# Bucketed attention and a wide feed-forward block on one core: the keyless share in the values' bank, a sum kept in PSUM, first products ahead of block transposes, and a hand-ordered last part

## The chip, the core and the metric

One core of one Trainium2 chip runs the whole program. The metric is device microseconds of one execution. TensorE (PE) multiplies, VectorE (DVE) and ScalarE (ACT) do elementwise work and read PSUM, GpSimd (POOL) works on SBUF alone, SyncE (SP) issues most DMAs. Each engine works through its own queue in order; waits between engines are semaphores.

## What is computed

Attention over 4 batches, 8 heads, 768 positions, head size 64, in which a query sees only the keys of its own hash bucket (six sign bits of a projection); then, with the heads joined to rows of 512, a normalised feed-forward block with 2048 hidden units and a residual.

```python
q_bits = (np.einsum('bhsd,dk->bhsk', q, proj) > 0)
k_bits = (np.einsum('bhsd,dk->bhsk', k, proj) > 0)
mask = q_bucket[:, :, :, None] == k_bucket[:, :, None, :]
scores = np.where(mask, scale * (q @ k.T), -1e9)
attn = np.exp(scores - max); attn = attn / (attn.sum(-1) + 1e-09)
x = heads_joined(attn @ v)
xn = (x - mu) / np.sqrt(var + 1e-06) * g_ln
out = x + np.maximum(xn @ w_ch1, 0.0) @ w_ch2
```

A query whose bucket holds no key sees all keys with equal weight (every score is -1e9). That is the share of keyless queries: the kernel gives every key a weight of 2^-100 beside the masked exponentials, which counts only where nothing else does.

## The kernel before

The work is cut into 12 chunks of 256 query rows (4 batches by 3). A chunk has two stages.

**Attention.** `att_units` (line 417) makes 12 units for a chunk: four pairs of heads, three units each. A unit is `scores` (S: 4 matmuls, line 446, into a two-bank tile of `ps_sc`, two of them), `exps` (one ACT instruction, line 456), `values` (A: 8 matmuls with the values and a column of ones, line 480, into the pair's tile `av`) and, after a pair's third unit, `divide` (lines 489 to 510) on DVE. The tile `av` is one bank of `ps_av`, and pairs take its two tags `av0` and `av1` in turn. For batch 0 the keyless share enters by a matmul (line 469). For batches 1 to 3 it is a tile `vsum` that `divide` adds: line 500 reads the sums of weights, line 501 adds `vsum` to the bank's numerators and writes the result to the SBUF tile `x`, line 506 takes the reciprocal, line 508 multiplies `x` by it in place.

**Feed-forward.** `mlp_steps` (line 516): `norm` (statistics with lines 527 and 528, centring with line 529, for the two row blocks in turn; then one DMA transpose on SP's queue, line 549, makes `xnT`), eight `up` steps (U: 8 matmuls, line 577, into a tile `hp`, then a rectification that goes to DVE, line 587, and ACT, line 589, by turns) and eight `down` steps (D: 4 matmuls, line 618; every fourth is followed by the residual on DVE, line 623, and the write of 128 rows). The tiles `hp`, `o2`, `hash` and `share` all take turns in the two banks of `ps_mm`: a new one waits until the reader of the one before last is done.

**Preparing the later batches**, by halves of four heads, on letters of a plan: L and W load, N casts to bfloat16 on POOL, B is four block transposes on DVE (line 287), T a DMA transpose, H the hash products (line 321), J spreads the bits by DMA, P shifts rows by DMA, V casts the values and sums them on POOL (lines 351 to 360), E is `share` (line 362): one matmul of the sums `vs16` into a bank of `ps_mm`, and a DVE copy into `vsum`.

**The order.** Chunks 0 and 1 are in a long list written out by hand. For chunks 2 to 11 the words of `steps[n]` (or `plain`) order the norm (`n`), the D steps (`d`), the U steps (`u`) and the preparation around the 12 units: chunk n's units run beside the norm and the U steps of chunk n-1 and the D steps of chunk n-2. `interleave` (line 692) places S of the next unit, then filler steps, then A, then fillers; a step's cost (U 900, D 870, H 1300, E 110, most others 0) decides where it lands. What costs 0 moves nothing on PE.

After chunk 11's units there remain the norm of chunk 11, eight D steps of chunk 10, eight U and eight D steps of chunk 11, the last four D steps split in two halves of columns (`down_columns`, line 596). That part is outside `manual_schedule`, so a scheduler orders each engine's queue. At the end each engine loads a flag (line 902) and branches (line 903) over a general path that these inputs do not need.

Of the kernel before, what the change touches and what calls it, by code (L numbers as in the profile page):

```python
# [9 lines left out]
F32 = mybir.dt.float32  # L10
# [20 lines left out]
def kernel(  # L31
# [11 lines left out]
    nc = tc.nc  # L43
    P = 128
# [102 lines left out]
    def load_values(b, half):  # L147
        h0 = half * H // 2
        eng = nc.gpsimd if (b, half) == (1, 0) else nc.sync
        if (b, half) == (0, 1):  # L150

            t = work.tile([P, NH * CT // 2], F32, tag="h", bufs=1, name="vnat1")[
                :, 0 : H // 2 * NC * D
            ].rearrange("p (h c d) -> p h c d", h=H // 2, c=NC)
        else:
            t = nat.tile([P, H // 2, NC, D], F32, tag="vnat", bufs=1, name="vnat")
        eng.dma_start(
            out=t, in_=v[b, h0 : h0 + H // 2].rearrange("h (p c) d -> p h c d", p=P)
        )
        return t  # L160

    class Prep:

# [197 lines left out]

        def share(self, half):

            ps = ps_mm.tile([P, H // 2 * D], F32, tag="mm", name="share")
            nc.tensor.matmul(ps, epsk, self.vs16.rearrange("p h d -> p (h d)"))
            nc.vector.tensor_copy(
                self.vs[:, half * H // 2 : (half + 1) * H // 2].rearrange("p h d -> p (h d)"), ps
            )
# [48 lines left out]
    def att_units(b, t, x):  # L417
# [15 lines left out]
        for j in range(NP):  # L433
            ha, hb = 2 * j, 2 * j + 1
            groups = [
                [(ha, 0), (ha, 1), (ha, 2), (ha, 3)],
                [(ha, 4), (ha, 5), (hb, 4), (hb, 5)],
                [(hb, 0), (hb, 1), (hb, 2), (hb, 3)],
            ]
            state = {}  # L440
            for g, grp in enumerate(groups):

                def scores(grp=grp, g=g, state=state):
                    sc = ps_sc.tile([P, 4, CT], F32, tag="sc", name="sc")
                    for i, (h, kj) in enumerate(grp):
                        nc.tensor.matmul(  # L446
                            sc[:, i, :],
                            key_block(h, kj),
                            query_blocks(h),
                        )  # L450
                    state["sc", g] = sc

                def exps(g=g, state=state):
                    sc = state["sc", g]
                    ex = work.tile([P, 4, CT], BF16, tag="ex", bufs=3, name="ex")
                    nc.scalar.activation(  # L456
                        ex, sc, AF.Exp,
                        bias=expb[:, 1:2] if b else expb[:, 0:1],
                        scale=scale if b else scale / Q_SCALE,
                    )  # L460
                    state[g] = ex

                def values(grp=grp, g=g, state=state, j=j, ha=ha):
                    if g == 0:
                        slot = 0 if (b, t) == (0, 0) else j % 2
                        av = ps_av.tile([P, 2, TT, D1], F32, tag=f"av{slot}", name="av")
                        state["av"] = av
                        if b == 0:
                            nc.tensor.matmul(
                                av,  # L470
                                epsk,
                                vsplit[:, ha : ha + 2, :].unsqueeze(2).to_broadcast(
                                    [P, 2, TT, D1]
                                ),
                                start=True, stop=False, skip_group_check=True,
                            )
                    av = state["av"]
                    for i, (h, kj) in enumerate(grp):
                        for qi in range(TT):
                            nc.tensor.matmul(  # L480
                                av[:, h - ha, qi, :],
                                state[g][:, i, qi * P : (qi + 1) * P],
                                va[:, h, kj, :],
                                start=(b > 0 and (g, i, qi) == (0, 0, 0)),
                                stop=(g == 2 and i == 3),
                                skip_group_check=True,
                            )

                def divide(g=g, state=state, ha=ha):
                    if g == 2:  # L490
                        av = state["av"]
                        rc = work.tile([P, 2, TT], F32, tag="rc", name="rc")
                        xv = x[:, :, ha * D : (ha + 2) * D].rearrange(
                            "p t (h d) -> p h t d", h=2
                        )
                        num = av[:, :, :, 0:D]
                        if b == 0:
                            nc.vector.reciprocal(rc, av[:, :, :, D])
                        else:
                            nc.vector.tensor_scalar_add(rc, av[:, :, :, D], S * EPS_KEY)  # L500
                            nc.vector.tensor_tensor(  # L501
                                xv, num,
                                vs[:, ha : ha + 2, :].unsqueeze(2).to_broadcast([P, 2, TT, D]),
                                op=AOP.add,
                            )
                            nc.vector.reciprocal(rc, rc)
                            num = xv
                        nc.vector.tensor_tensor(  # L508
                            xv, num, rc.unsqueeze(3).to_broadcast([P, 2, TT, D]), op=AOP.mult
                        )  # L510

                units.append((scores, exps, values, divide))
# [3 lines left out]
    def mlp_steps(b, t, x):  # L516
        st = {}
        steps = []

        def norm_rows(i):  # L520

            if i == 0:
                st["xn"] = work.tile([P, ND, TT, P], BF16, tag="xn", bufs=1, name="xn")
                st["mv"] = work.tile([P, TT, 2], F32, tag="mv", name="mv")
            xn, mv = st["xn"], st["mv"]
            stats = work.tile([P, 6], F32, tag="stats", bufs=4, name="stats")
            nc.vector.bn_stats(stats, x[:, i, :])  # L527
            nc.vector.bn_aggr(mv[:, i, :], stats)  # L528
            nc.vector.scalar_tensor_tensor(  # L529
                xn[:, :, i, :],  # L530
                x[:, i, :].rearrange("p (o d) -> p o d", d=P),
# [10 lines left out]

        def norm():

            for i in range(TT):
                norm_rows(i)
            if b or t > 1:
                xnT = work.tile([P, ND, CT], BF16, tag="xnT", bufs=1, name="xnT")
                nc.sync.dma_start_transpose(
# [17 lines left out]
            st["xnT"] = work.tile([P, ND, CT], BF16, tag="xnT", bufs=1, name="xnT")  # L567
            nc.vector.tensor_copy(st["xnT"], st["tp"])

        def up_products(n2):  # L570
            if n2 == 0:
                st["h"] = work.tile([P, NH, CT], BF16, tag="h", bufs=1, name="hbuf")
            hp = st["hp", n2] = ps_mm.tile([P, 2, CT], F32, tag="mm", name="hp")
            for i in range(2):
                nt = 2 * n2 + i
                for dt in range(ND):
# [36 lines left out]
        def down(i, part):  # L613
# [20 lines left out]
            (870, lambda i=i, part=part: down(i, part)) for i in range(TT) for part in range(4)  # L634
        ]
        parts = {
            "rows": norm_rows, "scale": norm_scale, "xt": xtrans, "xe": xcopy,
            "up": up_products, "relu": rectify, "columns": down_columns,
        }

# [106 lines left out]
    def first_two():  # L747
# [32 lines left out]
        def both(i):  # L780
# [22 lines left out]
            "su": lambda half: prep.sum_products(half),  # L803
            "sd": lambda half: prep.split_sums(half),
            "w": loads,
            "n": lambda i: parts["rows"](i),
            "nr": lambda _: parts["scale"](),
            "xt": lambda _: parts["xt"](),
            "xe": lambda _: parts["xe"](),
# [15 lines left out]

    steps = {
# [8 lines left out]
    }  # L835
    plain = "n d d d d d d d d u u u u u u u u"
    singly = {
# [9 lines left out]
    def sequence(text, norm, downs, ups, xtrans):  # L847

        downs, ups, out = list(downs), list(ups), []
        for word in text.split():  # L850
# [15 lines left out]
                out.append(parts_left[word].pop(0))  # L866
            else:
                out += prepare(word)
        assert not downs and not ups
        return out  # L870

    with tc.manual_schedule():
# [19 lines left out]
            interleave(units[n], fillers, after, single)  # L892
    tc.no_sync_barrier()
    norm, ups, downs, _, parts = mlp_steps(*chunks[-1], xs[len(chunks) - 1])
    for _, f in [norm] + tail + ups + downs[: 4 * (TT - 1)]:
        f()
    for lo in range(0, d_model, d_model // 2):
        parts["columns"](TT - 1, lo, lo + d_model // 2)
    main.close()


    ok = nc.values_load(flag[0:1, 0:1], min_val=0, max_val=1)
    with tc.If(ok < 1):
        general_path(
            tc, q, k, v, proj1, gbc, n_bits, w1_sb, w2_sb, identf, ident, out,
        )
# [192 lines left out]
```

## Time and profile before

| | us |
|---|---|
| median of 3 runs | 314.43 (313.21 to 315.44) |
| the profiled execution | 312.45 |
| its span, first to last instruction | 310.6 |

| engine | busy us | share of the span |
|---|---|---|
| PE | 299.4 | 96% |
| ACT | 217.2 | 70% |
| DVE | 184.6 | 59% |
| POOL | 84.7 | 27% |

Chunk 2's units begin at about 50 us, chunk 11's end at 285.7. The granted clock of PE is 1.0 throughout. The view of stages shows how full each engine is where the change acts (columns: us, then busy time of PE, its weight loads, DVE, ACT, POOL; granted clock; DMA share; GB/s):

```profile
core 0: us, PE busy (x) PEld busy (x) DVE busy (x) ACT busy (x) POOL busy (x), PEclk, DMA share, GB/s
75.00:98.00 23.00, 22.56 (x244) 17.32 (x244) 14.77 (x32) 18.13 (x24) 8.10 (x10) 1.00 0.62 168
98.00:123.00 25.00, 24.72 (x287) 18.86 (x288) 15.52 (x34) 19.45 (x27) 8.84 (x10) 1.00 0.55 139
171.00:195.00 24.00, 23.67 (x271) 17.89 (x273) 16.47 (x35) 18.30 (x25) 9.28 (x10) 1.00 0.57 133
285.70:310.60 24.90, 21.24 (x142) 13.80 (x142) 9.72 (x19) 2.76 (x5) 1.71 (x2) 1.00 0.19 57
```

### The profile page before, as it was taken

Reading aid. Unit: us, or ns where it says so; the run is one execution under the profiler, and the core shown is the slowest. Engines: PE = TensorE matmul, PEld = TensorE weight load, DVE = VectorE, ACT = ScalarE, POOL = GpSimd, SP = SyncE. Lnnn points to the kernel's source line nnn. Section 1 sums busy time; section 2 is a strip of 40 time slices with the busy share of each in tenths; the row PEclk is TensorE's granted clock in tenths of the full one; section 3 lists DMA queues with packets and bytes.
Section 4 is the critical chain, followed back from the end, with each engine's and each line's share of the span. In section 5 each row is a group of like instructions: output and inputs, shape, how many; then the busy total and the mean of one; then the engine's idle time right before and its main releaser. Section 6 shows DMA issues by size and latency. Waiting matters only on the chain.

```text
span 310.6 us, 7810 instructions
## 1 busy us (share of the span) xinstructions
PE 299.4 (96%) x3241; PEld 226.0 (73%) x3268; DVE 184.6 (59%) x404; ACT 217.2 (70%) x272; POOL 84.7 (27%) x110
## 2 busy tenths in 40 slices
PE   7979999999999999999999999999999999999995
PEld 6656787678669678678679668669679678688574
DVE  1799996654665756743793694653643734734522
ACT  5677977775798777688788778778778677666020
POOL 3467530914321118151290470100100100100200
PEclk9999999999999999999999999999999999999999
DMA  7999998487396476695199637030030110200302
GB/s 237 374 208 304 211 339 129 103 124 185 52 313 156 93 245 119 130 273 154 64 262 154 171 76 168 19 76 37 1 102 0 35 71 0 69 36 0 104 0 77
DMA packets 64970, 40.93 MB, mean 132 GB/s; under 512 B 47153, under 2 KB 59953, under 8 KB 64929
## 3 DMA queue, kind: packets, MB, share of 16 engines
q1 hardware_dynamic: 60224, 31.59, 41.1%
q0 software_dynamic: 4128, 8.13, 11.1%
q10 hardware_dynamic: 576, 0.66, 0.6%
q8 instruction: 27, 0.44, 0.6%
q14 instruction: 15, 0.11, 0.1%
HBM read 27.98 MB, written 6.88 MB: 112 GB/s over the span
## 4 chain that ended last, share of the span: by engine, by line
PE 84%; DVE 9%; ACT 3%; issue 2%; DMA 1%; POOL 0%; SPq 0%; ACTq 0%; POOLq 0%
PE hp L577 26%; PE o L618 22%; PE sc L446 18%; PE av L480 10%; PE hash L321 3%; DVE slots L262 2%; PE tpose L200 1%; DVE slots L238 1%; DVE bt L287 1%; PE wakep L762 1%; PE o L600 1%; PE hash L252 1%; DMA xnT<-xn 1%; DVE xn L529 1%; DVE x L508 1%
## 5 line engine op out<-in xcount | busy, mean ns | idle before, releaser
L456 ACT ACTIVATE ex<-sc,expb 128x1024 bf16<-128x1024 f32 x144 | 159.5, 1113 | 56.5 <-PE sc L446 54.0
L577 PE MATMUL hp<-xnT,w_sb 128*128 128x256 bf16 x768 | 98.7, 272 | 1.6 <-DVE hbuf L587 0.9
L618 PE MATMUL o<-w_sb,hbuf 128*128 128x512 bf16 x341 | 89.6, 379 | 1.2
L446 PE MATMUL sc<-slots 70*128 70x256 bf16 x576 | 86.5, 272 | 2.2 <-POOL slots L238 1.5
L577 PEld LDWEIGHTS <-w_sb 128*128 128x128 bf16 x768 | 72.0, 97 | 11.2 <-issue 2.4
L480 PEld LDWEIGHTS <-ex 128*128 128x128 bf16 x1152 | 54.0, 98 | 15.7 <-ACT ex L456 1.6
L446 PEld LDWEIGHTS <-slots 70*128 70x128 bf16 x576 | 51.8, 97 | 17.2 <-issue 3.7
L480 PE MATMUL av<-vaug,ex 128*128 128x65 bf16 x1152 | 58.8, 194 | 0.3 <-ACT ex L456 0.2
L587 DVE TENSOR_SCALAR hbuf<-hp 128x512 bf16<-128x512 f32 x48 | 32.8, 684 | 43.6 <-PE hp L577 42.5
L618 PEld LDWEIGHTS <-hbuf 128*128 128x128 bf16 x368 | 33.6, 97 | 25.5
L540 POOL TENSOR_SCALAR rs<-mv 128x2 f32<-128x2 f32 x12 | 9.1, 759 | 155.2 <-DVE mv L528 155.2
L589 ACT ACTIVATE hbuf<-hp 128x512 bf16<-128x512 f32 x48 | 28.5, 594 | 20.2 <-PE hp L577 20.2
L623 DVE SCALAR_TENSOR_TENSOR x<-o,rs,x 128x512 f32<-128x512 f32 x23 | 17.1, 744 | 26.4 <-PE o L618 23.5
L529 DVE SCALAR_TENSOR_TENSOR xn<-x,mv,gbc 128x512 bf16<-128x512 f32 x24 | 17.9, 751 | 0.8
L508 DVE TENSOR_TENSOR x<-x,rc 128x256 f32<-128x256 f32 x36 | 16.8, 466 | 1.2
L500 DVE TENSOR_SCALAR rc<-av 128x4 f32<-128x4 f32 x36 | 5.7, 158 | 19.8 <-PE av L480 19.8
L527 DVE BATCH_NORM_STATS2 stats<-x 128x6 f32<-128x512 f32 x24 | 16.5, 690 | 0.4
L351 POOL CAST vaug<-vnat 128x1536 bf16<-128x1536 f32 x8 | 12.0, 1494 | 15.6 <-DMA vnat<-in_v_dram 15.6
L501 DVE TENSOR_TENSOR x<-av,vsum 128x256 f32<-128x256 f32 x36 | 14.9, 414 | 0.0
L282 POOL CAST nat<-qnat 128x1536 bf16<-128x1536 f32 x6 | 8.8, 1470 | 16.8 <-issue 8.8
L180 ACT ACTIVATE knat<-knat 128x768 f32<-128x768 f32 x16 | 13.4, 836 | 0.0
L180 ACT ACTIVATE qnat<-qnat 128x768 f32<-128x768 f32 x16 | 13.3, 833 | 0.0
(86 smaller groups left out, 215.9 us busy)
## 6 DMA issues: line engine op xcount, KB each, us to landing
out_dram<-x SPq DMA_DIRECT2D x23, 256.0 KB
vnat<-in_v_dram SPq DMA_DIRECT2D x7, 768.0 KB
qnat<-in_q_dram SPq DMA_DIRECT2D x11, 384.0 KB
knat<-in_k_dram SPq DMA_DIRECT2D x11, 384.0 KB
w_sb<-in_moe_w_ch_dram POOLq DMA_DIRECT2D x4, 1024.0 KB, 14.4
slots<-slots SPq DMA_DIRECT2D x6, 384.0 KB
qnat<-in_q_dram POOLq DMA_DIRECT2D x2, 768.0 KB, 14.8
knat<-in_k_dram POOLq DMA_DIRECT2D x2, 768.0 KB, 16.0
```

Of the source, the lines that this page charges most:

```text
L180: nc.scalar.activation(src, src, AF.Square, accum_out=sq[:, a, col : col + 1],)
L446: nc.tensor.matmul(sc[:, i, :], key_block(h, kj), query_blocks(h),)
L456: nc.scalar.activation(ex, sc, AF.Exp, bias=expb[:, 1:2] if b else expb[:, 0:1], scale=scale if b else scale / Q_SCALE,)
L480: nc.tensor.matmul(av[:, h - ha, qi, :], state[g][:, i, qi * P : (qi + 1) * P], va[:, h, kj, :], start=(b > 0 and (g, i, qi) == (0, 0, 0)) ...
L508: nc.vector.tensor_tensor(xv, num, rc.unsqueeze(3).to_broadcast([P, 2, TT, D]), op=AOP.mult)
L527: nc.vector.bn_stats(stats, x[:, i, :])
L529: nc.vector.scalar_tensor_tensor(xn[:, :, i, :], x[:, i, :].rearrange("p (o d) -> p o d", d=P), mv[:, i, 0:1], gbc.rearrange("p (o d) -> p ...
L577: nc.tensor.matmul(hp[:, i, :], w1_sb[:, dt, nt * P : (nt + 1) * P], st["xnT"][:, dt, :], start=(dt == 0), stop=(dt == ND - 1),)
L587: nc.vector.tensor_scalar_max(dst, src, 0.0)
L589: nc.scalar.activation(dst, src, AF.Relu)
L618: nc.tensor.matmul(o2, st["h"][:, nt, i * P : (i + 1) * P], w2_sb[:, nt, :], start=(nt == 0), stop=(nt == NH - 1),)
L623: nc.vector.scalar_tensor_tensor(x[:, i, :], o2, st["rs"][:, i : i + 1], x[:, i, :], op0=AOP.mult, op1=AOP.add,)
```

## The change

Six edits:

1. `share` writes its product into the `av` tag that the latest pair does not hold, not into `ps_mm`.
2. For batches 1 to 3 the sum of numerators and `vsum` is written back to the PSUM bank and multiplied from there; `x` is written once.
3. In the plans of chunks 3, 4 and 7 some U steps stand ahead of the block transposes B; chunk 11 leaves its eighth U step out of the interleaving.
4. The norm is split into `row_stats` and `row_centred`, and for the last chunk both statistics come before both centrings.
5. The last part is ordered by hand: first the products of chunk 10's eighth U step, then the last norm, then the D steps of chunk 10, then the eight U steps, of which every second takes its tile from `ps_sc`, so that four are there.
6. A branch hint (LikelyTaken) is put on DVE and ACT for the branch over the general path. In the queues it stands behind chunk 11's last division on DVE and ahead of the last five rectifications on ACT.

PE's queue has the same instructions; up to chunk 10 they stand in the same order. On DVE, line 501's successor now waits for line 500's successor (both use the bank), the reciprocal no longer waits, and in the last norm the order is statistics, aggregate, statistics, aggregate, centring, centring, where the scheduler had put both statistics ahead of both aggregates. The queues of POOL and SP are unchanged.

```diff
         def share(self, half):
-            ps = ps_mm.tile([P, H // 2 * D], F32, tag="mm", name="share")
+            ps = ps_av.tile([P, H // 2 * D], F32, tag=f"av{1 - pair_bank[-1]}", name="share")
...
                         av = ps_av.tile([P, 2, TT, D1], F32, tag=f"av{slot}", name="av")
+                        pair_bank.append(slot)
...
                             nc.vector.tensor_tensor(
-                                xv, num,
+                                num, num,
                                 vs[:, ha : ha + 2, :].unsqueeze(2).to_broadcast([P, 2, TT, D]),
                                 op=AOP.add,
                             )
                             nc.vector.reciprocal(rc, rc)
-                            num = xv
...
-            for i in range(TT):
-                norm_rows(i)
+            if (b, t) == (B - 1, NT - 1):
+                order = [(row_stats, 0), (row_stats, 1), (row_centred, 0), (row_centred, 1)]
+            else:
+                order = [(row_stats, 0), (row_centred, 0), (row_stats, 1), (row_centred, 1)]
+            for step, i in order:
+                step(i)
...
-        def up_products(n2):
+        def up_products(n2, wide=False):
...
-            hp = st["hp", n2] = ps_mm.tile([P, 2, CT], F32, tag="mm", name="hp")
+            pool, tag = (ps_sc, "sc") if wide and n2 % 2 else (ps_mm, "mm")
+            hp = pool.tile([P, 2, CT], F32, tag=tag, name="hp")
+            st["hp", n2] = hp
...
-        3: "n L20 d d d d W20 d E11 d N20 d N20 B20 d T20 B20 u B20 u B20 u P20 u u u u u",
-        4: "n L21 d d d H20 d J20 d d N21 d N21 B21 d T21 B21 V20 u B21 u B21 u P21 W21 u u u u u",
+        3: "n L20 d d d d W20 d E11 d N20 d N20 B20 d T20 u B20 u u B20 u u B20 P20 u u u",
+        4: "n L21 d d d H20 d J20 d d N21 d N21 B21 d T21 V20 u B21 u u B21 u u B21 P21 W21 u u u",
...
-        7: "n d d d H30 d J30 N31 d N31 B31 d T31 B31 E30 d B31 V31 d B31 u P31 u u u u u u u",
+        7: "n d d d H30 d J30 N31 d N31 B31 d T31 B31 E30 d B31 V31 d u B31 u P31 u u u u u u",
...
+        11: "n d d d d d d d d u u u u u u u",
...
-    for _, f in [norm] + tail + ups + downs[: 4 * (TT - 1)]:
-        f()
-    for lo in range(0, d_model, d_model // 2):
-        parts["columns"](TT - 1, lo, lo + d_model // 2)
+    held = mlp[len(chunks) - 2][4]
+    with tc.manual_schedule():
+        held["up"](NH // 2 - 1)
+        norm[1]()
+        held["relu"](NH // 2 - 1, nc.scalar)
+        for _, f in tail:
+            f()
+        for n2 in range(NH // 2):
+            parts["up"](n2, True)
+            parts["relu"](n2, nc.scalar if n2 % 2 else nc.vector)
+        for _, f in downs[: 4 * (TT - 1)]:
+            f()
+        tc.mark_branch_hint_location(
+            "general", "LikelyTaken", [nc.vector.engine, nc.scalar.engine]
+        )
+        for lo in range(0, d_model, d_model // 2):
+            parts["columns"](TT - 1, lo, lo + d_model // 2)
...
-    with tc.If(ok < 1):
+    with tc.If(ok < 1, label="general"):
```

More of the change, by code (lines that the diff above doesn't have):

```diff
@@ L160, in load_values @@
         return t
+    pair_bank = []
     class Prep:
@@ L518, in mlp_steps, with row_stats @@
         steps = []
-        def norm_rows(i):
+        def row_stats(i):
             if i == 0:
@@ L524, in norm_rows @@
                 st["mv"] = work.tile([P, TT, 2], F32, tag="mv", name="mv")
-            xn, mv = st["xn"], st["mv"]
+            mv = st["mv"]
             stats = work.tile([P, 6], F32, tag="stats", bufs=4, name="stats")
@@ L528, in norm_rows, with row_centred @@
             nc.vector.bn_aggr(mv[:, i, :], stats)
+        def row_centred(i):
+            xn, mv = st["xn"], st["mv"]
             nc.vector.scalar_tensor_tensor(
@@ L636, in mlp_steps @@
         parts = {
-            "rows": norm_rows, "scale": norm_scale, "xt": xtrans, "xe": xcopy,
+            "stats": row_stats, "centred": row_centred, "scale": norm_scale, "xt": xtrans, "xe": xcopy,
             "up": up_products, "relu": rectify, "columns": down_columns,
@@ L805, in first_two @@
             "w": loads,
-            "n": lambda i: parts["rows"](i),
+            "n": lambda i: (parts["stats"](i), parts["centred"](i)),
             "nr": lambda _: parts["scale"](),
@@ L868, in sequence @@
                 out += prepare(word)
-        assert not downs and not ups
+        assert not downs
         return out
```

## The prediction

> **What bounds the kernel now.** I read the page's busy times first, then the chain of waits over the whole span, then the places where the chain leaves PE. PE is busy 96% of the span at a granted clock of 1.0. The chain gives prices for work that doesn't wait: a U step (8 products) 0.87 us, a D step (4) 0.86, S (4) 0.43, A (8) 0.26. A U step that starts later than its predecessors' prices allow is a stall. Five places before the last part show one (columns: start, us, what):
>
> ```profile
> 70.93 0.70 DVE hbuf L587
> 71.67 1.03 PE hp L577 x8
> ...
> 92.03 0.66 DVE hbuf L587
> 92.74 1.03 PE hp L577 x8
> ...
> 113.94 0.89 DVE bt L287
> 115.38 0.96 DVE bt L287
> 116.97 1.03 PE hp L577 x8
> ...
> 142.35 1.11 ACT ex L456
> 144.00 1.03 PE hp L577 x8
> ...
> 184.39 0.89 DVE bt L287
> 185.84 0.96 DVE bt L287
> 187.42 1.03 PE hp L577 x8
> ```
>
> Each time a U step waits for a rectification that frees its bank, and at 116.97 and 187.42 that rectification stood behind block transposes (92.74 likewise: the timeline has a transpose at 91.13 for 0.98 ahead of the rectification at 92.03). The sixth stall is in the last part, where the norm of chunk 11 outlasts the D steps that cover it:
>
> ```profile
> 286.80 1.29 DVE stats L527 x2
> 288.22 1.41 DVE xn L529 x2
> 289.69 3.07 DMA xnT<-xn
> 292.81 7.44 PE hp L577 x64
> ```
>
> Summing over starts of consecutive matmuls from 45 us on, what exceeds these prices and isn't a missing record comes to some 2.5 us. That is about all that PE can win there.
>
> **The share in the values' bank.** Before, the share's bank comes between two U tiles, so the next U waits for the last one's rectification. Six shares are made; the timeline shows two that cost time, at 70.98 and 143.66, both right after a pair's last A.
> - 70.98: the share takes 0.11 (the pace of 0.87/8), so U could start at 71.09, not 71.67: 0.58 won. But the bank that the share now takes is the next pair's. That pair's first matmul (line 469) would come at 71.09+0.87+0.43 = 72.39; the copy to vsum ends at 72.09+0.41 = 72.50, and PE starts 0.05 after a DVE release (71.62 to 71.67). So 0.16 goes back: net -0.42.
> - 143.66: U could start at 143.77, not 144.00: 0.23 won. The next pair's A would then come at 144.64; the copy ends at 144.79, 0.115 later by the slower division below, so A starts at 144.95: 0.31 lost. Net +0.08. Behind that A in PE's queue wait a U and the next S, so all of PE waits, ACT with its unit of slack does not.
> - The other four lie inside a pair, with at least one A step and 1.5 us ahead of the next pair: 0.
>
> **The sum in PSUM.** 36 divisions change. The add must now wait for line 500, which reads the same bank. Before, the two overlap (285.72 for 0.16, then 285.80); a waiting instruction starts 0.035 after its predecessor's end (line 506 ends at 286.30, line 508 starts at 286.34). So 0.16+0.035-0.08 = 0.115 more per division. No row before shows DVE writing PSUM. Reading it costs nothing:
>
> ```profile
> L508 DVE TENSOR_TENSOR x<-x,rc x36: 424/425/1080, 85.0 to 286.3; 128x256 f32<-128x256 f32 x36
> L508 DVE TENSOR_TENSOR x<-av,rc x12: 423/424/425, 20.4 to 78.6; 128x256 f32<-128x256 f32 x12
> ```
>
> The second row is batch 0's, from PSUM, the first from SBUF (min/median/max in ns). I take the write at 0, from the nearest rows: adds and copies of this size last 405 to 426 whatever they read. The bounds are -0.02 (the shortest of them) and +0.41 each (the time of the instruction again). It matters where a division is on the path, at 144 and in the last norm: up to +0.8 in all. Elsewhere 0.115 is covered: the tightest U step left at 163.03 has 0.22 between the rectification's end and its start. [...] What the edit gives back, the first row's tail up to 1080 ns (mean 466, 1.5 us over 36), falls in places where PE did not wait, but for about 0.05 at 183.92, which I leave out.
>
> **U steps ahead of B.** PE's order stays; only DVE's changes. Chunk 3: S at 91.80 lasts 0.43, U could start at 92.23, not 92.74: 0.51. Chunk 4: A at 116.44 and 0.26 give 116.70, not 116.97: 0.27. Chunk 7: 187.10, not 187.42: 0.32. With the rectification straight behind the division (ends 91.01) or the residual (115.46, 185.91) the banks are free 0.4 us and more before U needs them. Together -1.10. The last B is up to two U steps later, some 2.6 us; its reader, the hash product of chunk 4, comes at 105.55, the transposes end at 94.4, so 8 us hide it; without that cover PE would wait for whatever is left. P issues its DMA behind T's on SP's queue as before; V is POOL's, in the same order; neither queue changes.
>
> **The last part.** Count from the start of the last U inside chunk 11, 284.40 before. Before: U 0.87, A 0.25, D 32 x 0.215 = 6.88: PE is done at 8.00, and starts chunk 11's U at 292.81, 8.41. After, the same origin is 0.87 earlier (the eighth U comes later) and PE has 0.87+0.25+0.87+6.88 = 8.87 to do. The norm gets longer: the U in front of the last A is now the seventh, whose rectification is DVE's (0.69, ready 1.08 after the U's start, so the division waits until 1.69, not 1.32): +0.37. The division +0.115. Statistics: 0.69+0.035, aggregate 0.18 with 0.08 overlapped, and so on: the second centring ends 3.06 after the start, not 2.82: +0.24. So xnT lands at 8.36+0.73 = 9.09, U starts at 9.14, that is 8.27 by the old origin: -0.14. Bounds: -0.41 if DVE's additions don't show (PE's 8.87 rules), +0.27 if the write has its upper price.
> Four tiles for U: 64 products take 300.15-292.81 = 7.34 where 64 x 0.109 = 6.98 would do: -0.36; rectifications by two engines (0.69 and 0.60 per 1.74) keep up.
>
> **The hint.** Rows of the branch (min/median/max ns, start us):
>
> ```profile
> L903 PEldq COMPARE_BRANCH  x1: 3718/3718/3718, 305.7 to 305.7; - x1
> L903 DVEq COMPARE_BRANCH  x1: 72/72/72, 307.9 to 307.9; - x1
> L903 ACTq COMPARE_BRANCH  x1: 54/54/54, 308.8 to 308.8; - x1
> ```
>
> Only PE's is long; it ends at 309.47 and the trace's last landing of the output write is at 309.56, so it costs nothing, and PE gets no hint. DVE and ACT are done by 309.0. Hint: 0 (bounds 0 and the third rival).
>
> **Sum.** -0.42 +0.08 -1.10 -0.14 -0.36 = -1.94 against the profiled 312.45 (span 310.6 and 1.85 around it): 310.5. The median of the runs shown is 1.98 above the profiled one; I take off the same 1.94: 312.5.
>
> **Rivals.**
> 1. *The wait moves on.* The transposes, now spread among the U steps, stand ahead of later rectifications, and chunks 3, 4 and 7 stall two U steps later. For: each lasts 0.97, a rectification 0.68, against 1.74 for two U steps. Against: at 95.42 a U step with a like order around it had 0.42 to spare. It gives back the 1.10: 313.6.
> 2. *All covers hold.* No wait for vsum (-0.16-0.31), the norm hidden (-0.27), PE at its pace: -2.7, 311.7; with the scatter of a median (0.6, half the spread of the three runs) it can pass 1%. For: 1.5 us of DVE time come back. Against: the copy is last in a queue that the rows fix.
> [...]
>
> **Chances.** Forecast 0.69, first rival 0.14, second 0.10, third 0.07. A measurement of this kernel tells about 1% (3.1 us) from no change: faster is below 311.3, slower above 317.6. The forecast and first rival lie within; the second and scatter about the forecast put 0.15 below; the third with scatter, or with ACT stopping too, puts 0.05 above. The range: 311.7-0.6 = 311.1 below; above, the forecast with both upper prices, 313.3, and the first rival with scatter, 314.2. It leaves out the third rival and the tails.
>
> **What would show it.** In the profile after: U in chunks 3, 4 and 7 without a wait (right) or with one two steps later (first rival); line 469 and one A of chunk 5 waiting 0.1 to 0.3 for the vsum copy; the add row of 36 near 0.41; xnT landing 0.2 to 0.3 after PE's last D; 64 products in 7.0; the span near 308.7. A hole of 3 us on DVE after the last division, or PSUM adds near 0.8, would make it wrong.

## The result, and the profile after

The changed kernel took 312.60 us in the median (311.52 to 313.24, 11 runs), the kernel before, run on the same chip, 313.98 (313.21 to 315.67, 11 runs). The ratio is 0.9945 with a 95% interval of 0.9925 to 0.9965, that is 1.1 to 2.4 us less; the prediction took off 1.94. In the profiled execution the span is 309.8 us, where it was 310.6.

PE's chain after, at the places of the first fence of the prediction (start, us, what):

```profile
71.23 0.11 PE share L367
71.34 0.87 PE hp L589 x8
...
72.65 0.26 PE av L472
```

The U step at 71 us follows the share without a wait. The next pair's first matmul (line 472) starts 0.15 later than the pace of the starts before it would have it, for the copy to vsum.

```profile
84.19 0.07 DVE av L504
...
84.53 0.18 DVE rc L509
...
84.73 0.44 DVE x L510
...
85.31 0.27 PE share L367
```

This is a stretch of the same chain that was on PE before: the share at 85 us waits for the last instruction of the previous pair's division, which now reads its numerators from the bank that the share wants. The A before it starts at 84.69, so the share was due at 84.95; it comes 0.36 later, and PE waits with it.

The chain of the last part, which before went through the norm on DVE and the transposing DMA, is now PE alone; a wait of 0.14 for the norm is left between its second and third line, too short for the chain to leave PE:

```profile
283.93 0.87 PE hp L589 x8
284.81 6.91 PE o L630 x32
291.71 7.13 PE hp L589 x64
```

PE issues the same weight loads in the same order in both kernels up to chunk 11's units, so their starts can be laid side by side. The difference, after minus before:

| weight load of | before | after | after minus before | step |
|---|---|---|---|---|
| opening | 4.00 | 4.09 | +0.09 | |
| U after the first share | 71.68 | 71.17 | -0.50 | -0.59 |
| first values of the next pair | 72.98 | 72.64 | -0.35 | +0.15 |
| share of batch 1's second half | 85.26 | 85.27 | +0.01 | +0.36 |
| U in chunk 3 | 92.74 | 92.25 | -0.49 | -0.50 |
| U in chunk 4 | 116.97 | 116.27 | -0.70 | -0.21 |
| U after a share in chunk 5 | 144.00 | 143.07 | -0.94 | -0.24 |
| A after it | 144.88 | 144.26 | -0.61 | +0.33 |
| U in chunk 7 | 187.42 | 186.54 | -0.88 | -0.27 |
| last of the program | 306.88 | 305.41 | -1.47 | -0.59 |

PE is done 1.47 earlier, but the span is only 0.8 shorter. The rest went in the last write: its landing came 1.78 us after DVE's last residual before, and 2.42 after in this execution. Over the 14 profiled executions that time lies between 1.78 and 2.99 whatever the kernel. The runs' medians are not bound to this one execution, and their difference of 1.1 to 2.4 agrees with PE's 1.47.

### The profile page after: what moved, and what is told of

The parts are those of the page before. It is cut to its first block, busy times and chain, and to the rows that moved or that the text cites. A ratio compares the mean times of both kernels' runs of the same rounds, so it can differ in the third digit from the quotient of the medians.

```text
span 309.8 us, 7840 instructions
## 1 busy us (share of the span) xinstructions
PE 300.2 (97%) x3268; PEld 226.1 (73%) x3268; DVE 187.1 (60%) x404; ACT 217.1 (70%) x272; POOL 83.9 (27%) x110
## 4 chain that ended last, share of the span: by engine, by line
PE 90%; DVE 6%; ACT 2%; issue 1%; POOL 0%; POOLq 0%
PE hp L589 27%; PE o L630 25%; PE sc L448 18%; PE av L483 11%; PE hash L323 3%; DVE slots L264 2%; PE tpose L202 1%; DVE slots L240 1%; PE wakep L774 1%; PE o L612 1%; PE hash L254 1%; ACT qkT L219 1%; DVE x L510 1%; DVE xn L535 0%; DVE stats L529 0%
## 5 line engine op out<-in xcount | busy, mean ns | idle before, releaser
L630 PE MATMUL o<-w_sb,hbuf 128*128 128x512 bf16 x368 | 92.9, 379 | 0.0
L510 DVE TENSOR_TENSOR x<-av,rc 128x256 f32<-128x256 f32 x48 | 20.4, 424 | 1.6
L504 DVE TENSOR_TENSOR av<-av,vsum 128x256 f32<-128x256 f32 x36 | 15.6, 433 | 1.2
```

The lines of the kernel that those rows point to most:

```text
L510: nc.vector.tensor_tensor(xv, num, rc.unsqueeze(3).to_broadcast([P, 2, TT, D]), op=AOP.mult)
L630: nc.tensor.matmul(o2, st["h"][:, nt, i * P : (i + 1) * P], w2_sb[:, nt, :], start=(nt == 0), stop=(nt == NH - 1),)
```

## The experiments

Two measures are given for each. **PE's stretch** is the time from a fixed weight load in chunk 1 (it starts at 46.6 to 47.8, by how the opening went) to the start of PE's last matmul; it leaves the opening and the last landing out, and the two executions of an unchanged kernel (the change, the shares moved) differ by 0.04 or less where nothing collided. The **ratio** is that of the times to those of the kernel before in the same session.

| kernel | PE's stretch | ratio, 95% interval |
|---|---|---|
| before | 260.43 | 1 |
| the change | 258.89, again 258.92 | 0.9945 [0.9925, 0.9965], again 0.9936 [0.991, 0.9962] |
| plans only | 259.34 | 0.997 [0.9949, 0.9991] |
| share only | 259.95 | 0.998 [0.9952, 1.0009] |
| sum only | 260.69 | 1.0017 [0.9997, 1.0037] |
| end only | 260.50 | 0.9988 [0.9972, 1.0004] |
| change, sum in SBUF | 259.85, again 258.23 | 0.9932 [0.9903, 0.9961], again 0.9933 [0.9905, 0.9962] |
| change, no hint | 258.98 | 0.994 [0.9921, 0.9959] |
| change, two tiles | 259.25 | 0.9942 [0.992, 0.9964] |
| change, shares moved | 257.96, again 257.95 | 0.9921 [0.989, 0.9951], again 0.9906 [0.9879, 0.9933] |
| change, shares moved, sum in SBUF | 257.79 | 0.9902 [0.9875, 0.993] |

The intervals of the share, the sum and the end alone include 1, so what is said of these three rests on PE's stretch, in one profiled execution each.

The theory was that each edit is worth the PE stalls that it takes away or makes, and nothing else. The rivals were that the waits move on, that DVE's time lost against GpSimd is what pays, and that the hint does.

**Plans alone.** The kernel before with the plans of chunks 3, 4 and 7 of the change (the third edit, without chunk 11).

> The kernel before with only the plans of chunks 3, 4 and 7 changed (U steps ahead of block transposes). Theory (each edit is worth the PE stalls that it removes): U at 92.74, 116.97 and 187.42 starts without a wait; PE is 0.50, then 0.25, then 0.30 earlier, 1.05 in all at its last weight load; total -1.0 us, ratio 0.997. Rival (the wait moves on): chunks 3, 4 and 7 stall again within four U steps, PE ends under 0.4 earlier. Rival (what came back is DVE's time against GpSimd, so only the sum in PSUM counts): PE ends within 0.2 of before.

Measured: the U steps start 0.50, 0.28 and 0.33 earlier, and PE's stretch is 1.09 shorter; 0.3% less time. The chain of chunk 4, with the third U at 117.04 (start, us, what):

```profile
115.92 0.87 PE hp L577 x8
117.04 0.87 PE hp L577 x8
118.60 0.87 PE hp L577 x8
```

Each step is the price of a U, an A and perhaps an S apart; no wait comes back. The rival that the wait moves on falls.

**Share alone.** The kernel before with the first edit.

> The kernel before with only the share moved to the values' bank. Theory: -0.58+0.15 at 71 us; 0 at 85 us, because the bank is free after the add (line 501's successor), not after the multiplication; -0.24+0.20 at 144 us, as the division is not lengthened. PE ends 0.45 earlier, total -0.5, ratio 0.9985. Rival (the wait of 0.36 at 85 us belongs to the bank alone, not to the sum in PSUM): the share at 85 us waits 0.2 or more here too, and PE ends 0.1 to 0.2 earlier.

Measured: -0.58 and +0.15 at the first share, nothing at the second, -0.24 and +0.20 at the one in chunk 5: -0.47, as in the theory. The timeline at the second share (start, us, engine, line, what, count, idle before):

```profile
85.05 0.41 DVE L504 TENSOR_TENSOR x<-av,vsum 128x256 f32<-128x256 f32 x1
...
85.66 0.41 PE L483 MATMUL av<-vaug,ex 128*128 128x65 bf16 x8
...
85.91 0.27 PE L367 MATMUL share<-vs,epsk 128*128 128x256 bf16 x1
```

The add, the last that reads the bank here, is over at 85.46, before the A ahead of the share. So the wait of 0.36 belongs to neither edit alone: the share brings the bank into PE's path, and with the sum in PSUM the bank is free 1.15 after the division's start instead of 0.48.

**Sum alone.** The kernel before with the second edit.

> The kernel before with only the sum of numerators and share kept in PSUM. Theory: each division 0.13 longer (0.115 for the wait, 0.02 for the write), hidden everywhere but in the last norm, so PE ends 0.1 to 0.15 later; no multiplication over 0.43; total +0.1, ratio 1.000. Rival (GpSimd and DVE in each other's way is what the change removes): PE ends 0.8 or more earlier, ratio 0.997.

Measured: PE's stretch is 0.26 longer, twice what was expected. The last norm has 0.11 of it, as expected. The rest is +0.12 in chunk 4 and +0.07 in chunk 7, less 0.05 in chunk 3: the longer division is not hidden there, as it pushes the residual or the rectification that frees a U step's bank. The edit wins nothing on PE in this execution. The add into PSUM:

```profile
L501 DVE TENSOR_TENSOR av<-av,vsum x36: 432/433/433, 84.9 to 286.4; 128x256 f32<-128x256 f32 x36
```

That is 0.019 us more than the 0.414 (median of 36) of the add into SBUF. No multiplication is over 425 ns.

**The end alone.** The kernel before with chunk 11's plan, the hand-ordered last part, four tiles for U and the hint.

> The kernel before with only the end of the change: chunk 11's plan, the last part by hand with four tiles for U, the split norm and the hint. Theory: up to chunk 11 PE is as before; at its last weight load it is 0.7 earlier (0.36 by four tiles, 0.14 and 0.13 by the norm that lands no later than PE's last D step, some 0.1 by order); total -0.7, ratio 0.998. Rival (the hint is what pays): PE 0.3 earlier or less, the total -1 or more, the gaps after DVE's and ACT's branches gone.

Measured: from chunk 11 on PE wins 0.69, as expected. But the stretch is not shorter, 260.50: at 92.74 the U step that waits 0.50 in the kernel before waits 0.75 longer. The multiplication ahead of it lasted 1.37 instead of 0.42, beside a cast on GpSimd. In the kernel before the same multiplication had ended (91.02) just before the cast began (91.17). Here the opening was 1.25 later and with it the multiplication (from 91.85), but the cast, which waits for a load, only 0.3 (from 91.48): the multiplication began 0.37 into the cast. This was the first sign that what the prediction left out can be on the path.

**The sum back in SBUF, in the changed kernel.**

> The changed kernel with the sum of numerators and share written to SBUF again, as before. Theory (share and sum work against each other): the share at 85 us no longer waits (-0.36), the A at 144 us waits 0.2, not 0.33, the last norm is 0.13 shorter; PE ends 0.5 to 0.6 earlier than in the changed kernel, unless a cast on GpSimd falls on a multiplication just ahead of a rectification, which the early U steps now cover by 0.4. Total 0 to 0.5 below the changed kernel, ratio to before 0.993. Rival (the sum in PSUM pays, since multiplications blocked by GpSimd cost PE time): multiplications over 0.8 us come back and PE ends no earlier, or later, than in the changed kernel; ratio 0.995 to 0.997.

Measured in the first of two runs: 0.36 won at the second share, 0.12 at the A in chunk 5, 0.07 at a U step in chunk 7 and 0.09 in the last norm, but 0.63 and 0.97 lost in chunks 3 and 4, so that PE's stretch is 0.96 longer, as the rival had it. The timeline of chunk 3:

```profile
91.17 1.46 POOL L284 CAST nat<-qnat 128x1536 bf16<-128x1536 f32 x1 [7.20 <-DMA qnat<-in_q_dram]
91.29 1.63 DVE L511 TENSOR_TENSOR x<-x,rc 128x256 f32<-128x256 f32 x1
...
92.84 0.68 DVE L600 TENSOR_SCALAR hbuf<-hp 128x512 bf16<-128x512 f32 x1
```

The multiplication begins 0.12 into the cast and ends at 92.92, 0.28 after the cast's end at 92.64; so do the other two of this kind (in chunk 4: cast to 115.59, multiplication to 115.87; with the end alone: 92.95 and 93.23). In the seven executions with the sum in SBUF, all twelve multiplications that a cast lengthened end 0.27 to 0.28 after the cast, wherever in it they began. The rectification behind it, and the next U, wait. With both inputs, `x` and `rc`, in SBUF the multiplications that met a cast lasted up to 1.63; none lasts over 0.425 in the kernels that read the bank. Casts and multiplications met there too: in the seven executions with the sum in PSUM 31 multiplications began inside a cast, and each took 0.424 or 0.425. In the run without the hint one of them was the multiplication of chunk 3 (start, us, engine, line, what):

```profile
90.74 1.46 POOL L284 CAST nat<-qnat 128x1536 bf16<-128x1536 f32 x1 [7.65 <-DMA qnat<-in_q_dram]
...
90.89 0.42 DVE L510 TENSOR_TENSOR x<-av,rc 128x256 f32<-128x256 f32 x1
```

The same kernel was run again in a later session:

> The changed kernel with the sum in SBUF once more. The first look had a multiplication blocked by a cast on GpSimd at 91 and at 114 us, for 0.63 and 0.97 of PE time, against 0.64 won elsewhere. Theory (whether a cast falls on a critical multiplication is settled by when a load lands, so it differs from one execution to the next): this look may have 0, 1 or 2 such stalls; the times scatter more than the changed kernel's and their median is within 0.5 of it. Rival (they always meet): the same two stalls, the median 0.4 or more above the changed kernel.

In it no multiplication met a cast in chunks 3 and 4 (casts from 91.58 and 114.72, multiplications done at 91.45 and 113.88), and PE's stretch was 258.23, 0.66 shorter than the changed kernel's. So two executions of the same kernel are 1.6 apart. The times were expected to scatter more than the changed kernel's, and did not: 311.18 to 313.02 against 310.05 to 313.75. The times of both runs (ratios 0.9932 and 0.9933) cannot be told from the changed kernel's. The sum in PSUM buys insurance: it costs PE up to 0.66 where nothing collides, and saves 0.6 to 1 per collision. Which of the two weighs more over many executions stays open.

**No hint.** The mark and the label removed.

> The changed kernel without the branch hint. Theory: nothing moves; DVE's and ACT's branches last under 0.1, the gap after DVE's stays about 0.5, both done 1 us ahead of the last landing; ratio to before 0.9945, as with the hint. Rival (the hint pays): a branch or the gap after it on DVE or ACT grows by 2 us or more, and the total by 1 or more. Rival (the hint costs): 0.3 or more below the changed kernel.

Measured: stretch 258.98, ratio 0.994; DVE's branch lasts 72 ns and ACT's 54 without the hint, 84 and 68 with it. Nothing to win, nothing lost.

**Two tiles.** `parts["up"](n2)` in place of `parts["up"](n2, True)`.

> The changed kernel with chunk 11's U steps in two tiles again instead of four. Theory: waits of 0.14, 0.07, 0.07 and 0.07 return, 64 products take 7.34 instead of 6.99, total +0.35, ratio to before 0.9955. Rival (rectifications catch up anyway): 7.1 or less.

Measured: the 64 products take 7.43 instead of 7.13 in the chain, and PE's stretch is 0.36 longer; the times do not resolve it.

```profile
292.54 7.43 PE hp L589 x64
```

**Shares moved.** With the changed kernel's remaining waits known, the three shares at 72, 85 and 144 us were put where no pair has just ended, and both statistics of the last norm ahead of both aggregates:

```diff
-        2: "... u H11 u J11 E10 u V11 u u u u",
+        2: "... u H11 u J11 u u E10 V11 u u u",
-        3: "n L20 d d d d W20 d E11 d N20 ...",
+        3: "n L20 d d d d W20 d d E11 N20 ...",
-        5: "... E20 V21 d d u u u u E21 W30 u u u u",
+        5: "... E20 V21 d d u u u u u u E21 W30 u u",
```

> The changed kernel with the shares of batch 1 and the second of batch 2 moved by one or two steps, so that each lies inside a pair at least one unit after its first A, and with both statistics of the last norm ahead of both aggregates. Theory (what is left of waits is where share, division and next pair meet): the waits of 0.15 at 72 us, 0.36 at 85 us, 0.33 at 144 us and 0.14 at the last part's first U go; PE ends 0.95 earlier than in the changed kernel, ratio to before 0.9915. Rival (the wait moves on to the next user of the bank): PE ends under 0.4 earlier.

> The changed kernel with moved shares and both statistics first, once more. Theory: PE from chunk 2 to its last matmul 257.95, ratio to before 0.9915, 0.9 below the changed kernel. Rival (the end of the run hides it: the last landing scatters by over 1 us): less than 0.4 below the changed kernel.

Measured: 0.93 and 0.97 less in PE's stretch than the change; all four waits are gone, and PE has no wait over 0.12 left from chunk 2 to the end. In the second session, where the changed kernel ran beside it, the median is 311.00 (310.86 to 311.30, 6 runs) against 312.04 (310.05 to 313.75, 12 runs, ten of them above 311.30). It takes 0.9906 [0.9879, 0.9933] of the time of the kernel before. The last part's chain:

```profile
284.54 6.91 PE o L636 x32
291.44 7.04 PE hp L595 x64
```

U follows D with next to no wait for the norm (0.04).

> The moved shares with the sum in SBUF. Theory: PE has no wait on a share either way, the last norm is 0.13 shorter and hidden, so nothing is won; casts on GpSimd that meet a critical multiplication cost 0.5 to 1 each where they do. PE from chunk 2 on 257.95 to 259.5, time at or above the moved shares' with the sum in PSUM, ratio 0.9915 to 0.995. Rival (the sum in PSUM only costs): 0.3 or more below it.

Measured with the sum in SBUF besides: 257.79, which is below the expected range, and 0.16 less than with the sum in PSUM. So "nothing is won" was wrong: two U steps in chunks 4 and 7 start 0.07 and 0.06 earlier, and the last part 0.03. No cast met a multiplication on PE's path in this execution. The medians, 310.83 and 311.00, can't be told apart.

The changed kernel's second run, in the session of these three:

> The changed kernel once more, as the measure for the next three. Theory: PE's work from chunk 2 to its last matmul takes 258.9 again, ratio to before 0.9945; multiplications all under 0.43.

It came as expected: 258.92, ratio 0.9936, no multiplication over 425 ns.

## Why the prediction was right, step by step

| step | predicted | in the change | alone |
|---|---|---|---|
| share at 71 us | -0.42 | -0.44 | -0.43 |
| share at 85 us | 0 | +0.36 | 0 |
| share at 144 us | +0.08 | +0.09 | -0.04 |
| U ahead of B | -1.10 | -1.11 | -1.11 |
| sum in PSUM, at a U step in chunks 4 and 7 | 0 | +0.13 | +0.12 |
| last norm | -0.14 | -0.23 | |
| four tiles | -0.36 | -0.36 | |
| sum | -1.94 | -1.56 | |

(The norm in the change is -0.59 of the last part less the -0.36 that the two-tile run gives to the tiles. The opening's +0.09 makes -1.56 into -1.47. In the table of starts the +0.13 stands within the steps of chunks 4 and 7.)

The accounting by stalls held: the removed ones were read off the chain to within 0.1, and none came back two U steps later. But new stalls came, at one share and at two U steps, which the prediction had put at nothing, and the total is 0.4 short.

That 312.5 and 312.60 agree to 0.1 is in part luck. The forecast took 1.94 off a median of three runs, 314.43; the median of eleven is 313.98, 0.45 lower, and PE won 1.55 in its stretch, 0.4 less. The two misses cancel. The scatter of 0.6, called half the spread of the three runs, was also too small: their spread is 2.23, half of it 1.1.

The wait of the next pair for the copy came as worked out (0.16 predicted and 0.15 measured, 0.31 and 0.33). The price of the add into PSUM, taken as 0 between -0.02 and +0.41, is +0.019. The last norm holds PE up by 0.14 and not by the 0.27 of the prediction. Reading the numerators from PSUM cost nothing in the change either: the multiplication from the bank lasts 424 to 425 ns in all 48 cases, the one with both sources in SBUF 425 in the median before.

**What failed at a share.** "The other four lie inside a pair, with at least one A step and 1.5 us ahead of the next pair: 0." The step looked at who uses the bank next, and not at who used it last. The second share comes straight after a pair's first A (84.69) and takes the bank of the previous pair, whose last A started at 83.14. That pair's division starts only at 84.00, since a residual holds DVE. With the division 0.13 longer and its last read the multiplication, the bank comes free 0.36 too late. The run with the share alone shows 0 there, the changed kernel 0.36.

**What failed at two U steps.** "Elsewhere 0.115 is covered: the tightest U step left at 163.03 has 0.22 between the rectification's end and its start." This looked at U steps that wait for a rectification, but a residual frees a bank of `ps_mm` just so. One does in chunk 4 and one in chunk 7. Before:

```profile
114.75 0.71 DVE L623 SCALAR_TENSOR_TENSOR x<-o,rs,x 128x512 f32<-128x512 f32 x1
...
115.56 1.04 PE L577 MATMUL hp<-xnT,w_sb 128*128 128x256 bf16 x8
```

The residual ends at 115.46 and PE can start 0.05 later, so the cover is 0.05. In the change it is used up:

```profile
114.39 0.71 DVE L635 SCALAR_TENSOR_TENSOR x<-o,rs,x 128x512 f32<-128x512 f32 x1
...
115.15 1.03 PE L589 MATMUL hp<-xnT,w_sb 128*128 128x256 bf16 x8
```

U starts 0.05 after the residual's end at 115.10, with PE idle for 0.07 before it; at 185.43 it is the same. Both stalls are there in every profiled execution of the change and of the shares moved, at 0.07 each, and both are gone with the sum in SBUF (the second run of the change, and the shares moved).

**What was left out.** The multiplications blocked by casts were put aside since none of them held up PE in the profile of before. That was true of that execution, by 0.15 us. In 2 of the 7 profiled executions with the sum in SBUF, one or two of them cost PE 0.6 to 1.0 each.

The third rival, that the hint stops DVE, had 0.07 of the chances, and no run shows such a stop: in the change DVE goes on 0.04 after the last division (285.48 to 285.52), and with and without the hint PE's stretch agrees within 0.1. The second rival, worth 2.7, did not come about in the change; with the shares moved PE's stretch is 2.5 shorter than before.

## What to carry to other kernels

When a tile moves to another bank, look in both directions: who reads the bank last before it, as the same change may have lengthened that, and who writes it next. When an instruction gets longer, list every release behind it, of whatever kind, before calling it covered. In a kernel whose main engine is 96% busy, laying the starts of the same instruction of two executions side by side tells edits of 0.1 us apart where the times of ten runs don't tell 0.5. A wait that misses the path by 0.2 us in one profile is a cost with a chance, to be entered in the range.

## What the runs showed of the hardware

The landing of the last write of 128 KB took 1.78 to 2.99 us after the instruction that made its data, over 14 executions of 11 kernels in which that part hardly differs; it is more than most edits here are worth.

The opening differed by up to 1.25 us at 47 us, in code that no edit touched. In the run of the end alone, the granted clock fell there (columns as in the view of stages before):

```profile
24.00:28.00 4.00, 4.00 (x30) 1.94 (x28) 3.31 (x7) 3.14 (x3) 2.63 (x3) 0.57 1.12 261
28.00:32.00 4.00, 3.86 (x47) 2.73 (x45) 3.46 (x8) 1.96 (x3) 2.88 (x5) 1.00 1.06 344
```

PE did 30 matmuls in the first of these windows at a mean clock of 0.57 where the kernel before did 49 at 1.0. Of the 1.25 by which that run's opening was late, 0.43 was there before the clock fell, and the shares moved, in their second run, opened as late at a clock of 1.0; so a fall of the clock is not what openings differ by in general, and the rest stays open. A later opening, against loads that did not land later by as much, is what put the cast on the multiplication in that run.

PE's branch over the general path lasts 3.5 to 4.2 us in every kernel (3.72 before, 3.58 in the change) and ends 0 to 1.0 us before the last landing (0.09 before, 0.87 in the change); it would be next if that landing were made earlier by more than that.
